# Loading two weight matrices in a permuted row order, in half-size transfers

## The chip, the cores and the metric

One core of one Trainium2 chip. The time is device time in microseconds of one execution. A run is called slow when it is over 1.5% above the fastest of the same kernel. Five runs here are slow (one of e3, one of e9, three of e10); every ratio and every profile of a whole kernel is of fast runs alone. The runs of one batch were made on one chip beside runs of the kernel before. A ratio compares the fast runs of two kernels in the same rounds and comes with a 95% interval; it is therefore not quite the ratio of the medians that stand beside it.

## The reference

Causal attention over 4 batches, 8 heads, 768 positions and head size 64 (three heads attend to everything, five to four sink positions and a window of 64), and then on x of 3072 x 512, the heads side by side:

```
h1 = x @ w1            # w1, w2: 512 x 1024
h2 = x @ w2
g = np.maximum(h1, h2)
out = g @ w_out        # w_out: 1024 x 512
```

## The kernel before

Since max(h1, h2) = h2 + relu(x (w1 - w2)), the kernel computes relu(x wd) w_out + x (w2 w_out) with wd = w1 - w2. A planner written in Python orders the instructions of all engines by estimated costs. The parts that matter here (cuts marked):

```python
def load_weight(name, c, queue=nc.sync):
    ...
    else:
        rows, cols = quarter(c)                # 256 rows, 512 columns
    queue.dma_start(out=dst[:, rows, cols],
                      in_=arr[rows.start * 128:rows.stop * 128, cols].rearrange("(c p) f -> p c f", p=128))
...
# wd = w1 - w2, a quarter at a time, on VectorE or GpSimd
    nc.vector / nc.gpsimd .tensor_sub(out=wd_bf[at], in0=w_raw[0][at], in1=w_raw[1][at])      # shortened
...
# w2 is cast to bf16, transposed on TensorE (8 groups) and multiplied by w_out
    nc.tensor.transpose(psb[:, c * 128:(c + 1) * 128], w2_bf[:, c, fch * 128:(fch + 1) * 128], ident)
...
# the attention result of a head, divided by its sum, goes into 64 columns of x
    V.tensor_tensor(out=xs[b].t[:, n0:n0 + nn, bass.ds(col(s0 + h), D)], in0=p4[:, i, :, 0:D],
                    in1=rz_[:, i].unsqueeze(2).to_broadcast([128, nn, D]), op=ALU.mult)
...
# x (w1 - w2): waits for the quarters of wd that hold its columns
    nc.tensor.matmul(bk.t[:, 0, 0:GT], lhsT=wd_bf[:, c, f * 128:(f + 1) * 128], rhs=xt[b].t[...], ...)
```

The softmax here doesn't subtract the row's maximum and nothing guards it: scores larger than these inputs give would overflow.

## Time and profile before

| | before |
|---|---|
| median of 4 runs, us | 187.32 (187.02 to 188.51) |
| TensorE busy in the profiled run | 170.2 of 186.1 us |
| DMA engines | full until about 125 us, then mostly free |
| w1 and w2 | 8 transfers of 512 KB, 7.5 us from issue to landing |

The views that bound the kernel stand in the prediction. One view is added: the chain that ended last, in order of time (start, length, what), here its longer pieces that carry the weights.

```profile
23.03 8.34 DMA raw<-in_moe_w_dram
31.39 7.52 DMA raw<-in_moe_w_dram
...
43.59 7.38 DMA raw<-in_moe_w_dram
51.05 2.45 POOL wd_bf L443 x2
```

The last quarter of w1 lands, and GpSimd at once subtracts w2 from it. In GpSimd's list (start, length, what, idle time before it and what ended it) its last two subtractions end at 55.7 us:

```profile
51.05 4.67 POOL L443 TENSOR_TENSOR wd_bf<-raw 128x1024 bf16<-128x1024 f32 x2 [0.61 <-DMA raw<-in_moe_w_dram]
```

In the list of TensorE's instructions the first product that needs this half of wd starts at 55.77 us.

### The profile page before, as it was taken

What the parts mean: (1) busy time and instruction counts of PE and PEld (TensorE: products, weight loads), DVE (VectorE), ACT (ScalarE), POOL (GpSimd) and SP (SyncE); (2) the same over time, 40 slices, a digit from 0 to 9 for tenths busy, and PEclk for the clock granted to TensorE, in tenths of its full rate; (3) what the DMA queues carried; (4) which work ended last, traced back from release to release, by engine and by line L of the source; (5) the groups of instructions that cost most, each with busy time, mean ns of one, the idle gap of its engine ahead of it and who ended that gap; (6) DMA issues with size and microseconds to landing.
All of it is one profiled execution on the core that took longest, in us unless ns stands there. A gap on an engine that the chain in (4) does not pass through costs nothing.

```text
span 186.1 us, 4594 instructions
## 1 busy us (share of the span) xinstructions
PE 170.2 (91%) x1643; PEld 100.6 (54%) x1663; DVE 88.0 (47%) x250; ACT 115.8 (62%) x195; POOL 50.7 (27%) x108
## 2 busy tenths in 40 slices
PE   1969988799999999999999999999999999999990
PEld 1845755556755655665565466446555545545460
DVE  5567775768778486544478165354743000000000
ACT  2546998878887678717894386368844624426330
POOL 2101331456796865623025234200000000000000
PEclk9985999999999999999999999999999999999999
DMA  6999999999999899999999999994016612022022
GB/s 142 303 272 356 288 335 354 248 289 311 324 255 249 187 223 221 239 239 176 262 227 240 237 207 202 331 175 174 5 58 188 96 60 113 0 80 89 4 113 70
DMA packets 79553, 36.96 MB, mean 199 GB/s; under 512 B 68642, under 2 KB 73506, under 8 KB 79522
## 3 DMA queue, kind: packets, MB, share of 16 engines
q1 hardware_dynamic: 76130, 35.27, 76.7%
q10 hardware_dynamic: 3392, 1.31, 2.7%
q8 instruction: 15, 0.25, 0.6%
q14 instruction: 16, 0.13, 0.2%
HBM read 25.17 MB, written 6.29 MB: 169 GB/s over the span
## 4 chain that ended last, share of the span: by engine, by line
PE 67%; DMA 15%; issue 4%; SPq 3%; POOL 2%; DVE 2%; DVEq 0%; ACT 0%; POOLq 0%
DMA raw<-in_moe_w_dram 12%; PE mm L786 12%; PE mm L762 10%; PE po L762 7%; PE po L623 7%; PE mm L793 6%; PE sc L578 6%; PE po L786 5%; PE sc L786 4%; DMA ld<-in_q_dram 3%; PE po L793 3%; PE sc L762 2%; PE sc L793 2%; SPq L671 2%; PE mm L695 1%
## 5 line engine op out<-in xcount | busy, mean ns | idle before, releaser
L599 ACT ACTIVATE at_all<-sc 128x1024 bf16<-128x1024 f32 (+2 forms) x72 | 59.8, 869 | 7.3 <-PE sc L578 3.6
L301 POOL CAST qb<-ld 128x384 bf16<-128x384 f32 x51 | 24.5, 508 | 25.1 <-DVE at_all L610 16.9
L762 PEld LDWEIGHTS <-wd_bf 128*128 128x128 bf16 x256 | 23.2, 98 | 14.4 <-POOL wd_bf L443 0.4
L762 PE MATMUL mm<-xt,wd_bf 128*128 128x384 bf16 x136 | 26.8, 326 | 0.2 <-POOL wd_bf L443 0.2
L623 PE MATMUL po<-vb,at_all 128*128 128x65 bf16 x472 | 26.6, 196 | 0.3 <-POOL vb L301 0.2
L623 PEld LDWEIGHTS <-at_all 128*128 128x128 bf16 x472 | 21.9, 99 | 9.0 <-issue 1.4
L578 PE MATMUL sc<-qk 64*128 64x128 bf16 (+2 forms) x364 | 23.1, 240 | 2.2 <-POOL qk L301 0.8
L642 DVE TENSOR_TENSOR xs<-po,rz 128x192 f32 x64 | 22.9, 357 | 2.9 <-DVE rz L639 0.6
L786 PEld LDWEIGHTS <-raw 128*128 128x128 bf16 x152 | 14.2, 98 | 13.8
L578 PEld LDWEIGHTS <-qk 64*128 64x128 bf16 x364 | 12.6, 95 | 14.7 <-issue 10.2
L786 PE MATMUL mm<-wo_bf,raw 128*128 128x512 bf16 (+1 forms) x75 | 18.9, 368 | 0.3
L301 POOL CAST vb<-ld 128x384 bf16<-128x384 f32 (+1 forms) x30 | 13.5, 475 | 20.8 <-DMA ld<-in_v_dram 8.8
L639 DVE RECIPROCAL rz<-po 128x6 f32<-128x6 f32 x32 | 6.2, 193 | 26.0 <-PE po L623 26.0
L762 PE MATMUL po<-xt,wd_bf 128*128 128x384 bf16 x92 | 18.1, 326 | 0.0
L299 ACT COPY ot<-mm 128x512 f32<-128x512 f32 (+1 forms) x12 | 6.8, 567 | 13.2 <-PE mm L793 11.6
L610 DVE TENSOR_TENSOR at_all<-at_all,smk 128x1024 bf16<-128x1024 bf16 (+3 forms) x27 | 14.9, 571 | 0.0
L793 PEld LDWEIGHTS <-xt 128*128 128x128 bf16 x100 | 9.3, 98 | 9.3
L793 PE MATMUL mm<-wm_bf,xt 128*128 128x512 bf16 (+1 forms) x55 | 13.9, 371 | 0.1
L610 DVE TENSOR_TENSOR at_all<-at_all,tri 128x256 bf16<-128x256 bf16 (+1 forms) x36 | 10.1, 313 | 6.6 <-ACT at_all L599 6.5
L695 PEld LDWEIGHTS <-qb 128*128 128x128 bf16 x108 | 7.2, 103 | 5.0 <-DVE qb L301 2.6
L299 ACT COPY vb<-vb 4x256 bf16<-4x256 bf16 (+1 forms) x16 | 6.1, 380 | 6.2 <-PE po L623 6.1
L770 ACT ACTIVATE raw<-mm 128x384 bf16<-128x384 f32 x17 | 8.3, 490 | 2.5 <-PE mm L762 2.2
(91 smaller groups left out, 188.5 us busy)
## 6 DMA issues: line engine op xcount, KB each, us to landing
ld<-in_q_dram SPq DMA_DIRECT2D x32, 192.0 KB, 4.9
ld<-in_k_dram SPq DMA_DIRECT2D x32, 192.0 KB, 4.6
out_dram<-ot SPq DMA_DIRECT2D x23, 256.0 KB, 2.5
ld<-in_v_dram SPq DMA_DIRECT2D x24, 192.0 KB, 4.0
raw<-in_moe_w_dram SPq DMA_DIRECT2D x8, 512.0 KB, 7.5
raw<-in_moe_w_out_dram SPq DMA_DIRECT2D x3, 512.0 KB, 5.8
xt<-in_v_dram ACTq DMA_DIRECT2D x3, 256.0 KB, 3.4
ld<-in_v_dram SPq DMA_DIRECT2D x8, 96.0 KB, 4.3
```

The costliest lines, as they stand in the source:

```text
L299: nc.scalar.copy(out=o, in_=i)
L301: issued[e].append((V if e == "DVE" else nc.gpsimd).tensor_copy(out=o, in_=i).ins)
L578: nc.tensor.matmul(sc.t[:, k, off:off + w], lhsT=qk.t[64 * h:64 * h + 64, 1, j * 128:(j + 1) * 128], rhs=qk.t[64 * h:64 * h + 64, 0, q0:q0 ...
L599: nc.scalar.activation(out=a.t[:, k:k + m, 0:n], in_=sc.t[:, k:k + m, 0:n], func=ACT.Exp, scale=scale, bias=0.0 if bias is None else bias[ ...
L610: issued["DVE"].append(V.tensor_mul(out=y, in0=y, in1=z).ins)
L623: nc.tensor.matmul(po[u].t[:, 0, o:o + D + 1], lhsT=a.t[:, k, off + t * 128:off + (t + 1) * 128], rhs=vb.t[:, h, j, :], **fresh(u))
L642: V.tensor_tensor(out=xs[b].t[:, n0:n0 + nn, bass.ds(col(s0 + h), D)], in0=p4[:, i, :, 0:D], in1=rz_[:, i].unsqueeze(2).to_broadcast([128, ...
L695: nc.tensor.transpose(psb[:, n * 128:(n + 1) * 128], qb.t[:, i, n].rearrange("p h d -> p (h d)"), ident)
L762: nc.tensor.matmul(bk.t[:, 0, 0:GT], lhsT=wd_bf[:, c, f * 128:(f + 1) * 128], rhs=xt[b].t[:, g * NB // NG:(g + 1) * NB // NG, c, :], start ...
L770: nc.scalar.activation(out=gt.t[:, f, :], in_=bk.t[:, 0, 0:GT], func=ACT.Relu)
L786: nc.tensor.matmul(bk.t[:, 0, 0:m1 - m0], lhsT=gt.t[:, f, t * 128:(t + 1) * 128], rhs=wo_bf[:, f, m0:m1], start=(f == 0), stop=False)
L793: nc.tensor.matmul(bk.t[:, 0, 0:m1 - m0], lhsT=xt[b].t[:, c0 // 128, c, :], rhs=wm_bf[:, c, m0:m1], start=False, stop=(c == KC - 1))
```

## The change

The intent, as I read it: let the DMA engines read neighbouring rows of w1 and w2 at the same time. The 128 rows of a chunk are taken in a two-level order, 16 groups of 8, row 16 b + a to partition 8 a + b. The rows are what x is multiplied along, so the columns of x must be permuted alike; pcol, the column of x at which a head's result starts, is computed by VectorE at run time and gets a new formula. Each quarter becomes two transfers of 256 KB.

```diff
+        rows, cols = quarter(c)
+        for r in range(rows.start, rows.stop):
+            queue.dma_start(out=dst[:, r, cols],
+                            in_=arr[r * 128:(r + 1) * 128, cols].rearrange("(b a) f -> a b f", a=16))
...
-        for o, width_ in ((perm, 1), (pcol, D)):
-            V.tensor_scalar_mul(out=o[0:1, 0:H], in0=key[0:1, 2, :], scalar1=-float(H * width_))
+        V.tensor_scalar_mul(out=perm[0:1, 0:H], in0=key[0:1, 2, :], scalar1=-float(H))
+        V.tensor_scalar(out=pcol[0:1], in0=perm[0:1, 0:H], scalar1=1, scalar2=None, op0=ALU.bitwise_and)
+        V.tensor_scalar_mul(out=key[0:1, 1, :], in0=perm[0:1, 0:H], scalar1=16.0)
+        V.scalar_tensor_tensor(out=pcol[0:1], in0=pcol[0:1], scalar=-15.0, in1=key[0:1, 1, :], op0=ALU.mult, op1=ALU.add)
...
-                        V.tensor_tensor(out=xs[b].t[:, n0:n0 + nn, bass.ds(col(s0 + h), D)], in0=p4[:, i, :, 0:D],
-                                        in1=rz_[:, i].unsqueeze(2).to_broadcast([128, nn, D]), op=ALU.mult)
+                        V.tensor_tensor(out=xs[b].t[:, n0:n0 + nn].rearrange("p n (y w) -> p n y w", w=4)[
+                        :, :, bass.ds(col(s0 + h), 16, 2)], in0=p4[:, i, :, 0:D].rearrange("p n (e a) -> p n a e", a=16),
+                                    in1=rz_[:, i].unsqueeze(2).unsqueeze(3).to_broadcast([128, nn, 16, 4]), op=ALU.mult)
```

(The planner's cost of a weight transfer goes from 0.5 to 1.0 us of SyncE; the bounds and the other branch follow the new column numbers.)

More of the change, by code (lines that the diff above doesn't have):

```diff
@@ L307, in load_weight @@
             rows, cols = slice(c * FC // 4, (c + 1) * FC // 4), slice(0, d_model)
-        else:
-            rows, cols = quarter(c)
-        queue.dma_start(out=dst[:, rows, cols],
-                          in_=arr[rows.start * 128:rows.stop * 128, cols].rearrange("(c p) f -> p c f", p=128))
+            queue.dma_start(out=dst[:, rows, cols],
+                            in_=arr[rows.start * 128:rows.stop * 128, cols].rearrange("(c p) f -> p c f", p=128))
+            return
+        rows, cols = quarter(c)
+        for r in range(rows.start, rows.stop):
+            queue.dma_start(out=dst[:, r, cols],
+                            in_=arr[r * 128:(r + 1) * 128, cols].rearrange("(b a) f -> a b f", a=16))
     def quarter(c):
@@ L425, in run @@
                 else:
-                    d_w[name, c] = P.op(lambda e, name=name, c=c: load_weight(name, c), {"SP": 0.5},
+                    d_w[name, c] = P.op(lambda e, name=name, c=c: load_weight(name, c), {"SP": 0.5 if name == "wo" else 1.0},
                                         prio=LATER[name, c], size=0.524, rate=0.35)
@@ L831 @@
     if not narrow:
-        run([True] * H, lambda s: s, lambda s: s * D, False)
+        run([True] * H, lambda s: s, lambda s: 32 * (s // 2) + s % 2, False)
         return
@@ L840 @@
         _, xcol = nc.values_load_multi_w_load_instructions(
-            pcol[0:1, 0:H], engines=(mybir.EngineType.DVE,), min_val=0, max_val=(H - 1) * D,
+            pcol[0:1, 0:H], engines=(mybir.EngineType.DVE,), min_val=0, max_val=32 * (H // 2 - 1) + 1,
             skip_runtime_bounds_check_because="a permutation of the heads")
@@ L844 @@
     with branch.Else():
-        run([True] * H, lambda s: s, lambda s: s * D, False)
+        run([True] * H, lambda s: s, lambda s: 32 * (s // 2) + s % 2, False)
         with tc.manual_schedule():
```

## The prediction

> **What bounds the kernel now.** I read four views, in this order: the busy times and the forty slices (what is full, and when), the stretches of time (how much TensorE idles in each part), the waits (what it idled for), and the DMA issues. First the page's busy line and slices (each digit is the busy share of 4.65 us in tenths):
>
> ```profile
> PE 170.2 (91%) x1643; PEld 100.6 (54%) x1663; DVE 88.0 (47%) x250; ACT 115.8 (62%) x195; POOL 50.7 (27%) x108
> ...
> PE   1969988799999999999999999999999999999990
> ...
> DMA  6999999999999899999999999994016612022022
> ```
>
> Two resources are full. TensorE is near nine tenths or above from the second slice to the end. The sixteen DMA engines are full from the second slice until about 125 us, then mostly free. The last third is dense matrix work with no loads to wait for. To put numbers on it I cut the span into stretches (length, then busy time and instructions of each engine, granted clock, DMA share, GB/s):
>
> ```profile
> 0.00:25.00 25.00, 17.86 (x203) 13.36 (x205) 15.93 (x57) 14.94 (x24) 5.44 (x23) 0.86 0.94 270
> 25.00:35.00 10.00, 7.58 (x117) 4.96 (x116) 7.13 (x17) 8.68 (x15) 1.23 (x4) 1.00 1.01 335
> 35.00:60.00 25.00, 24.41 (x299) 15.62 (x299) 18.91 (x48) 20.85 (x32) 18.30 (x29) 1.00 1.01 285
> 60.00:130.00 70.00, 69.36 (x708) 39.09 (x715) 38.16 (x109) 46.35 (x79) 25.68 (x56) 1.00 1.10 224
> 130.00:180.50 50.50, 50.23 (x324) 27.09 (x326) 7.86 (x21) 24.21 (x47) 0.00 (x0) 1.00 0.24 71
> ```
>
> TensorE idles 7.14 us before 25 us (4.19 of it before its first instruction), 2.42 us in 25 to 35, 0.59 in 35 to 60, 0.64 in 60 to 130 and 0.27 in 130 to 180.5. After 35 us a better transfer can return 1.5 us at most; the whole room in which weights can matter is 25 to 60 us, 3.0 us of idle time, 1.6% of the span. The waits of TensorE (total us, times, longest) say what these were:
>
> ```profile
> PE mm L401 <- DVE pcol L347: 4.2, 1, 4.2
> PE mm L695 <- DVE qb L301: 1.9, 3, 0.8
> PE mm L452 <- DVE w_bf L301: 0.9, 1, 0.9
> PE sc L578 <- POOL qk L301: 0.8, 1, 0.8
> ...
> PE mm L762 <- POOL wd_bf L443: 0.2, 1, 0.2
> ```
>
> Only the third and the last concern w1 and w2: 1.1 us. The first matters for another reason: nothing starts before VectorE has written pcol, and the diff makes pcol longer. The chain that ended last seems to contradict this small room:
>
> ```profile
> DMA raw<-in_moe_w_dram 12%; PE mm L786 12%; PE mm L762 10%; PE po L762 7%; PE po L623 7%; PE mm L793 6%; PE sc L578 6%; PE po L786 5%; PE sc L786 4%; DMA ld<-in_q_dram 3%; PE po L793 3%; PE sc L762 2%; PE sc L793 2%; SPq L671 2%; PE mm L695 1%
> ```
>
> 12% is 23 us of weight transfers on the chain. But they lie at 23.0 to 38.9 and 43.6 to 51.0 us, and in 35 to 60 TensorE was busy 24.41 of 25 us with other work. A chain names one sequence of releases; it does not say that TensorE stood still. I therefore do not take the 23 us as a gain to be had.
>
> [...] That is the motive I read into the diff: today neighbouring groups of partitions read w rows many 4 KiB pitches apart, and after it index a, the outermost, steps through adjacent rows. The trace of before does not show such a loss at this pitch. Its packet records give every 2,048-byte packet 84 ns in the median, for w1 and w2, for w_out (2 KiB rows, no gaps) and for the output alike. The means are 102.6 ns for the packets of 22.6 to 52 us (2,048 of w1 and w2, 256 of w_out) and 105 for the three w_out transfers before. [...] The new write of x puts runs of four bf16, 8 bytes,[...]; no row of before has this pattern. [...]
>
> **The change part by part.**
>
> ```profile
> L642 DVE TENSOR_TENSOR xs<-po,rz 128x192 f32 x64 | 22.9, 357 | 2.9 <-DVE rz L639 0.6
> ...
> L301 DVE COPY qk<-po 128x768 bf16<-128x768 bf16 x3 | 2.9, 954 | 1.7 <-PE po L623 0.9 <-POOL vb L301 0.8
> ...
> L301 DVE COPY xt<-po 128x768 bf16<-128x768 bf16 x1 | 0.6, 557 | 0.0
> ```
>
> *The multiply that writes x.* Same 64 instructions and 192 elements, but PSUM is read with steps of 16 floats in runs of four. The copy to qk reads PSUM with its innermost step over 256 bytes and takes 954 ns for 768 elements[...]; the copy to xt, which is contiguous, takes 557[...]. I expect 357 ns to stay, within 20 ns: 64 x 0.02 = 1.3 us at most, on an engine 47% busy. Nothing on the end.
>
> *The prologue.* Before, perm and pcol are two independent scalings starting 3.52 and 3.60 us into the trace and ending by 3.75. After, pcol is an AND of perm, a scaling of perm, and a combination: two instructions more, two dependent steps. Dependent small VectorE steps start 0.19 us apart here (2.88, 3.07, 3.26; 3.34 to 3.52), so AND at 3.71, scaling at 3.79, combination at 3.98, end at 4.13: 0.37 us later. The first load issues and TensorE's first instruction wait for it, so about +0.35 us on the path; a part may hide behind the w_out transfer already in the queue. I take +0.3.
>
> *The issues.* The page's issue rows (size, median time to landing):
>
> ```profile
> raw<-in_moe_w_dram SPq DMA_DIRECT2D x8, 512.0 KB, 7.5
> raw<-in_moe_w_out_dram SPq DMA_DIRECT2D x3, 512.0 KB, 5.8
> ```
>
> Eight issues become sixteen of 256 KB. One costs SyncE's queue about 0.47 us when it is not held, so 8 x 0.47 = 3.8 us more, spread over 21 to 47 us. In that stretch the queue was held by full DMA engines: issues of 2.71 us for two at 28.0, 2.88 for one at 31.4 and 2.68 for two at 43.6, against 0.47 each, which is 1.8 + 2.4 + 1.7 = 5.9 us of slack. The additional issues fit inside it. I take 0 for the end, with up to +0.5 if a q load falls behind.
>
> *The transfers.* Bytes, packet size and number of packets stay. The 7.5 us to landing is mostly backlog: 0.5 MB at about 300 GB/s is 1.7 us. The most that a better order can give is the mean falling to the median, (102.6 - 84) x 2,048 / 16 engines = 2.4 us of DMA time. As only 1.1 us of TensorE's idling was for these weights, and the excess looks the same for w_out, I take a tenth to a half of that: -0.3 us.
>
> *The schedule.* The kernel's own planner now reckons 1.0 us of SyncE for a weight transfer in place of 0.5. In its model the transfer itself takes 0.524/0.35 = 1.5 us, so the DMA stays the limit of its plan and the order should change little; a few swaps may shift the time by some tenths either way.
>
> Sum: 187.37 + 0.3 + 0 - 0.3 +- swaps = 187.4 us.
>
> **The rivals.** *Transfers were held by row conflicts, and the order frees them.* For it: the 23 us on the chain, 7.5 against 5.8 us to landing, packets of up to 1.08 us. Against it: the 84 ns median and the equal means. If the packets fell to 84 ns and all of the 1.1 us of weight waits and half of the other 25-to-35 us idle time went, the gain were about 1.8 us: 185.6. *The new grouping makes transfers slower.* [...] packets could near twice 84 ns, 2,048 x 84 / 16 = 10.8 us more DMA time before 52 us. TensorE would fill part of that with attention and lose perhaps 3 to 5 us: 190 to 192. Against it: nothing in before shows it, and how a 16 x 8 order is dealt to engines I cannot see. *VectorE becomes slower with the strided pattern*: at 200 ns more each, 12.8 us of VectorE work, of which perhaps 2 us in the first 60 us, where it is busy 17 of 25, delay TensorE: 189.
>
> **Range and chances.** The centre is 187.4. The first rival sets the low end, 185.6; half of the second's and all of the third's loss set the high end, 189.6. Faster by over 2% needs under 183.6, more than the 3.0 us of idle time before 60 us: 0.03. Slower by over 2% is above 191.1[...]: 0.08. Within 2%: 0.89.
>
> **What would show it.** Right: L642 stays at 357 ns; pcol ends about 0.37 us later and the first q load is issued that much later; sixteen weight issues with held issues shortened; 2,048-byte packets still 84 ns in the median; idle time of TensorE in 25 to 60 us between 2 and 3.5 us. Wrong: a packet median above 100 ns[...], a mean near 84 with weights landing earlier and the idle time under 1.5 us (conflicts), L642 above 400 ns, or an order of instructions that differs much on TensorE.

## The result

The changed kernel takes 193.97 us in the median of 4 runs (192.25 to 194.81) against 187.32 before: ratio 1.0341 (1.0264 to 1.0418). It is slower by 3.4%, outside the range on record. The result is correct.

The stretches of time of the kernel after (columns as in the prediction):

```profile
0.00:25.00 25.00, 17.99 (x204) 13.18 (x205) 16.47 (x59) 14.78 (x24) 5.75 (x22) 0.86 0.89 265
25.00:35.00 10.00, 7.68 (x114) 4.75 (x111) 5.17 (x12) 7.89 (x14) 0.75 (x3) 1.00 1.00 254
35.00:60.00 25.00, 21.59 (x247) 14.30 (x246) 17.10 (x38) 17.13 (x25) 13.38 (x22) 0.86 1.08 250
60.00:130.00 70.00, 68.33 (x702) 38.35 (x701) 41.53 (x114) 45.56 (x76) 30.32 (x60) 1.00 1.13 231
```

The last two columns tell the cause's place. In 25 to 35 us the DMA engines are as full as before (share 1.00 against 1.01), yet move 254 GB/s and not 335; in 35 to 60 us 250 and not 285. Full engines that move less are engines whose packets take longer: the weight packets took 122 ns in the median against 84, as counted below. TensorE idles 3.41 us in 35 to 60, where it had idled 0.59, and its granted clock there is 0.86: the record of the clock shows half of full speed for 6.8 us from 35.8 us on. Its waits:

```profile
PE mm L460 <- DVE w_bf L301: 2.7, 1, 2.7
...
PE mm L771 <- POOL wd_bf L451: 1.6, 1, 1.6
PE po L631 <- DVE xs L650: 1.2, 1, 1.2
```

The wait for the cast of w2 went from 0.9 to 2.7 us, that for wd from 0.2 to 1.6, and a new one stands on the multiply that writes x, which follows casts of late weights in VectorE's order. The multiply itself, and the page's row of weight transfers:

```profile
L650 DVE TENSOR_TENSOR xs<-po,rz 128x192 f32 x64 | 22.9, 357 | 2.8 <-DVE rz L647 0.6
...
raw<-in_moe_w_dram SPq DMA_DIRECT2D x16, 256.0 KB, 6.8
```

The multiply is as long as before. A transfer of half the size takes 6.8 us to land where the whole took 7.5; in e1 below, halves in plain order land in 4.9. The chain in order of time:

```profile
26.73 9.36 DMA raw<-in_moe_w_dram
36.11 6.94 DMA raw<-in_moe_w_dram
43.06 7.01 DMA raw<-in_moe_w_dram
...
53.70 6.62 DMA ld<-in_q_dram
...
60.51 2.35 POOL wd_bf L451
```

The chain names a q load before the last subtraction, but GpSimd's list shows that its two last subtractions run back to back and that w1 ended the wait before them:

```profile
58.20 4.65 POOL L451 TENSOR_TENSOR wd_bf<-raw 128x1024 bf16<-128x1024 f32 x2 [1.47 <-DMA raw<-in_moe_w_dram]
```

So it is the chain of before, later: GpSimd's last subtraction ends at 62.86 us, and the first product that needs it starts at 62.91, 7.14 us later than before. I then measured, in the profiled runs of the whole kernel, how long TensorE still works from this product to the start of its last instruction:

| run | transposes of w2, 5th group, us | that product of x wd, us | from there to TensorE's last start, us |
|---|---|---|---|
| before | 34.68 | 55.77 | 125.25 |
| after | 37.84 | 62.91 | 125.11 |
| e1_split | 34.29 | 55.11 | 124.88 |
| e3_form16far | 38.02 | 62.84 | 125.11 |
| e9_only_w2 | 37.77 | 59.61 | 124.88 |
| e11_only_w1 | 34.31 | 59.09 | 125.10 |
| e6_groups4 | 36.67 | 58.84 | 125.10 |
| e10_form4 | 35.00 | 56.57 | 125.24 |

The last column is constant within 0.4 us (in e2, e4 and e8, not in the table, it is 125.06, 124.88 and 125.24), so the column before it decides the time of the profiled run. The packet records of the two traces, counted over all weight packets of 2,048 bytes from 22.5 to 60 us (2,048 of w1 and w2, 256 of w_out), give the size: the median goes from 84 to 122 ns and the mean from 102 to 129. That is (129.0 - 102.3) x 2,304 / 16 engines = 3.8 us of DMA time. The packets of q and k (1,536 bytes), whose transfers the change does not touch, rise from 20.8 to 23.9 us of DMA time over the whole trace, 3.2 us more; of this 2.7 us (8.4 to 11.1) fall between the first and the last weight packet. Together 6.5 to 7.0 us, beside the 7.1 by which the product is late. This is an account of sizes and not a proof: the first weight packet also started 1.1 us later (22.65 and 23.72 us).

### The profile page after: what moved, and what is told of

It is laid out like the page before. It is cut to its first block, busy times and chain, and to the rows that moved or that the text cites.

```text
span 193.0 us, 4632 instructions
## 1 busy us (share of the span) xinstructions
PE 173.9 (90%) x1663; PEld 102.1 (53%) x1663; DVE 91.3 (47%) x252; ACT 116.1 (60%) x195; POOL 50.8 (26%) x108
## 4 chain that ended last, share of the span: by engine, by line
PE 65%; DMA 18%; SPq 5%; POOL 2%; issue 2%; DVE 1%; DVEq 0%; ACT 0%; POOLq 0%
PE mm L795 12%; DMA raw<-in_moe_w_dram 12%; PE mm L771 10%; PE po L771 7%; DMA ld<-in_q_dram 6%; PE po L631 6%; PE mm L802 6%; PE sc L586 6%; PE po L795 5%; PE sc L795 4%; SPq L315 4%; PE po L802 3%; PE sc L771 2%; PE sc L802 2%; PE mm L704 1%
## 5 line engine op out<-in xcount | busy, mean ns | idle before, releaser
L301 POOL CAST vb<-ld 128x384 bf16<-128x384 f32 (+1 forms) x30 | 13.7, 479 | 23.7 <-DMA ld<-in_v_dram 11.1
L795 PE MATMUL mm<-wo_bf,raw 128*128 128x512 bf16 (+1 forms) x80 | 19.4, 368 | 0.0
L647 DVE RECIPROCAL rz<-po 128x6 f32<-128x6 f32 x32 | 6.2, 193 | 24.1 <-PE po L631 23.9
L618 DVE TENSOR_TENSOR at_all<-at_all,tri 128x256 bf16<-128x256 bf16 (+1 forms) x36 | 12.5, 380 | 6.7 <-ACT at_all L607 6.6
L704 PEld LDWEIGHTS <-qb 128*128 128x128 bf16 x108 | 7.7, 106 | 6.0 <-DVE qb L301 2.5
```

Source lines behind the costliest of these rows:

```text
L301: issued[e].append((V if e == "DVE" else nc.gpsimd).tensor_copy(out=o, in_=i).ins)
L618: issued["DVE"].append(V.tensor_mul(out=y, in0=y, in1=z).ins)
L704: nc.tensor.transpose(psb[:, n * 128:(n + 1) * 128], qb.t[:, i, n].rearrange("p h d -> p (h d)"), ident)
L795: nc.tensor.matmul(bk.t[:, 0, 0:m1 - m0], lhsT=gt.t[:, f, t * 128:(t + 1) * 128], rhs=wo_bf[:, f, m0:m1], start=(f == 0), stop=False)
```

## The experiments

Three things changed in the transfers at once: their number, which rows are read together, and the form of the source order. Theory P supposes that the form, 16 groups of 8 partitions, makes the packets slow, because DMA engines then hinder each other at the partitions they write; e7 calls it the port theory. Theory H supposes that neighbouring rows, read at once, collide in HBM, the memory that the inputs lie in. S says that the number of transfers costs it, X that the writing of x does. For every kernel of the whole-kernel experiments the order of TensorE's instructions was compared with that of before and is the same (e8 has its added products besides). Before itself took 186.57 us in the median in the batch of e1 to e4, 187.20 in that of e6 to e9, and 186.99 in that of e10 and e11.

### e1_split: the number of transfers alone

```diff
+        for r in range(rows.start, rows.stop):
+            queue.dma_start(out=dst[:, r, cols], in_=arr[r * 128:(r + 1) * 128, cols])
```

> The kernel before with nothing but each weight transfer cut in two (256 KB each, rows in their natural order, sixteen issues as in the changed kernel); right results. Theory P[...] and theory H (neighbouring rows are read at once and collide in HBM) both expect about 187.5 us, 2,048-byte packets of the weights near 84 ns in the median and 24 us idle of nothing new. Theory S (sixteen transfers of half the size cost it: more issues[...]) expects 193 to 195 us with packets still at 84 ns.

Measured: correct, 186.61 us (186.14 to 187.68), ratio 0.999 (0.9921 to 1.0059). Packets 84 ns in the median, mean 99, and a transfer lands in 4.9 us. Eight more issues cost nothing that can be seen: all sixteen take SyncE 9.2 us, the eight of before 9.4. S falls.

### e2_xonly: the columns of x and the prologue alone

```diff
 # the changed kernel with the load of before
+        queue.dma_start(out=dst[:, rows, cols],
+                        in_=arr[rows.start * 128:rows.stop * 128, cols].rearrange("(c p) f -> p c f", p=128))
```

> The changed kernel with the weights loaded as before (eight transfers, natural row order); the columns of x stay permuted, so the result is wrong on purpose. P, H and S expect 187.0 to 188.0 us, the multiply that writes x at 357 ns. Theory X (the strided write of x and the longer pcol cost it) expects 193 to 195 us.

Measured: wrong, 187.33 us (187.11 to 188.05), ratio 1.0035 (0.9975 to 1.0096). The multiply takes 357 ns here too. X falls as the cause; a cost of some tenths of a per cent is neither shown nor excluded.

### e3_form16far: the two-level order, rows far apart

```diff
 # e1 with another source: group a starts 7 rows after group a-1
+  bass.AP(tensor=arr.tensor, offset=r * 128 * d_ff + cols.start, ap=[[7 * d_ff, 16], [d_ff, 8], [1, d_ff // 2]])
```

> Sixteen transfers as in e1, but each source is a two-level order of 16 groups of 8 rows, group a starting 7 rows after group a-1 and its 8 rows following one another, so that groups lie 28 KiB apart and not 4 KiB as in the changed kernel; wrong result on purpose (rows 7 a + b). P expects the loss of the changed kernel, 193 to 195 us, with weight packets of 105 to 140 ns in the median. H expects about 187.5 us and 84 ns.

Measured: wrong, 193.9 us in the median of 6 (192.68 to 195.67, one of them slow; 193.03 without it), ratio 1.0314 (1.0238 to 1.039). Packets 118 ns in the median. This is the whole loss, with the groups 28 KiB apart and not 4. TensorE's waits are those of after:

```profile
PE mm L455 <- DVE w_bf L301: 3.0, 1, 3.0
PE mm L765 <- POOL wd_bf L446: 1.8, 1, 1.8
```

### e4_near128: neighbouring rows, plain order

```diff
 # e1 with another source: one level, 1 KiB from partition to partition
+  bass.AP(tensor=arr.tensor, offset=r * 128 * d_ff + cols.start, ap=[[d_ff // 4, 128], [1, d_ff // 2]])
```

> Sixteen transfers as in e1 in the plain one-level order over 128 partitions, but with a step of 1 KiB and not 4 KiB from partition to partition[...]; wrong result on purpose. P expects about 187.5 us and packets of 84 ns. H expects 193 to 195 us and packets of 105 to 140 ns.

Measured: wrong, 187.04 us (186.27 to 187.6), ratio 0.9993 (0.9932 to 1.0055), packets 84 ns, mean 98.5. Together e3 and e4 decide between P and H: the form (16 groups of 8) costs the time, and the distance of the rows does not. H falls as the cause of this loss for the distances tried: 4 and 28 KiB from group to group (122 and 118 ns a packet), 4 and 1 KiB from partition to partition (84 ns both). How the form does it is not shown by them.

### e5_alone: transfers with nothing beside them

Eight loads of one form at a time, each batch waiting for the last. This is one execution, its state unknown.

> No attention and no products: eight loads of 256 KB (128 KB for low) of w1 at a time, with nothing beside them, in nine forms one after another; wrong result on purpose. nat and tail are the plain order; adjs is that of the changed kernel (16 groups of 8, groups 4 KiB apart); fars has groups 28 KiB apart; near is the plain order with a 1 KiB step; low fills partitions 0 to 63 alone; gfour is 32 groups of 4, gtwo 64 groups of 2; same has all 16 groups read the same 8 rows. P expects nat, near and tail at 84 ns a packet, some 360 GB/s; adjs, fars, gfour and same slow alike, 105 to 150 ns; low[...] slow too[...]; gtwo between. H expects adjs and near slow, same the slowest, fars at 84 ns.

Measured: packet medians of 84 ns for nat, near and tail, 119 for adjs and 118 for same, as P expected. In the steady middle of a batch adjs starts about 65 packets per half microsecond, near about 89. Three expectations were missed. The median of fars is 84 ns (above 100 in parts of its batch, mean 110, against 118 for adjs). That is what H expected and not P; near at 84 ns speaks against H all the same. In the whole kernel the two distances hardly differ (e3 118 ns, after 122), so a small effect of the distance beside that of the form stays open. gfour and gtwo have a median of 84 ns and a 90th percentile of 84 and 85: a two-level order is not slow as such, groups of eight are (adjs and same here, e3 in the kernel). And low has 84 ns, but its issues limited it: 128 KB per issue, and an issue took 0.62 us. A by-product is the cost of an issue, from SyncE's list (start, length of all eight, what):

```profile
9.68 3.65 SPq L36 DMA_DIRECT2D nat<-in_moe_w_dram  x8
19.79 5.14 SPq L40 DMA_DIRECT2D adjs<-in_moe_w_dram  x8
...
49.76 4.99 SPq L52 DMA_DIRECT2D low<-in_moe_w_dram  x8
57.23 5.10 SPq L56 DMA_DIRECT2D gfour<-in_moe_w_dram  x8
```

Over all 128 partitions a two-level source takes 5.14/8 = 0.64 us to issue, a plain one 0.46. The two levels are not all that counts: low has a plain source too, to 64 partitions, and takes 0.62.

### e6_groups4: the same idea with groups of four rows

```diff
-  arr[r * 128:(r + 1) * 128, cols].rearrange("(b a) f -> a b f", a=16)
+  arr[r * 128:(r + 1) * 128, cols].rearrange("(b a) f -> a b f", a=32)     # x in runs of 2, pcol = 32 perm - 31 (perm & 1)
```

> The changed kernel with 32 groups of 4 rows in place of 16 groups of 8: row 32 b + a goes to partition 4 a + b, and the columns of x follow; sixteen transfers in two-level order as in the changed kernel, right result. If groups of eight partitions[...] (theory P, narrowed after e5, where groups of 4 and 2 kept 84 ns), this takes 186.5 to 188 us with packets at 84 ns. If any two-level order, or its dearer issue (0.63 us against 0.46 in e5), costs the time, it takes 192 to 195 us.

Measured: correct, 189.39 us in the median of 6 (188.54 to 190.84), ratio 1.0107 (1.0077 to 1.0137). Packets are back at 84 ns, mean 105 (102 before). Both expectations missed: two thirds of the loss are gone, and 1.1% stays.

### e7_ports: the partitions

The transfers alone again, of whole 4 KiB rows, to chosen partitions; one execution, its state unknown.

```diff
+    batch("mids", 32, 64, [[3 * W, 16], [W, 4]], 64)     # 16 groups of 4, to partitions 32 to 95
+    batch("lows", 0, 64, [[3 * W, 16], [W, 4]], 64)      # the same to partitions 0 to 63
```

> Transfers alone again, now of whole 4 KiB rows so that issues do not limit them; wrong result on purpose. mids and lows are the same 16 groups of 4 rows, to partitions 32 to 95 and 0 to 63; midp and lowp the same in plain order; eight is 16 groups of 8 on 128 partitions, four 32 groups of 4, plain the plain order. The port theory expects[...] mids near 165 ns a packet of 4 KiB and 390 GB/s while it runs steadily[...], lows[...], lowp like lows, midp like mids, eight between (200 to 280 ns), four and plain near 165. If it is the slowest dimension of 16 that is slow, mids, lows and eight are slow alike and lowp is not.

Measured, 4,096-byte packets:

| batch | order, partitions | median ns | mean ns |
|---|---|---|---|
| mids | 16 groups of 4, 32 to 95 | 159 | 192 |
| lows | 16 groups of 4, 0 to 63 | 324 | 302 |
| midp | plain, 32 to 95 | 159 | 187 |
| lowp | plain, 0 to 63 | 318 | 296 |
| eight | 16 groups of 8, all 128 | 272 | 260 |
| four | 32 groups of 4, all 128 | 159 | 180 |
| plain | plain, all 128 | 159 | 194 |

The page's rows of transfers say the same in us to landing:

```profile
eight<-in_moe_w_dram SPq DMA_DIRECT2D x6, 512.0 KB, 8.5
four<-in_moe_w_dram SPq DMA_DIRECT2D x6, 512.0 KB, 6.9
plain<-in_moe_w_dram SPq DMA_DIRECT2D x6, 512.0 KB, 6.1
...
mids<-in_moe_w_dram SPq DMA_DIRECT2D x6, 256.0 KB, 4.1
lows<-in_moe_w_dram SPq DMA_DIRECT2D x6, 256.0 KB, 5.2
midp<-in_moe_w_dram SPq DMA_DIRECT2D x6, 256.0 KB, 4.0
lowp<-in_moe_w_dram SPq DMA_DIRECT2D x6, 256.0 KB, 4.9
```

mids and lows differ in nothing but the partitions, and the packets of lows take twice as long: 324/159 = 2.04. The plain orders lowp and midp show the same, 318 and 159 ns. P expected lows and lowp to be the slow ones. So in this run it was the 64 partitions written that decided what a packet cost, in either order. The rival, that a slowest dimension of 16 is slow as such, falls: mids has it and keeps 159 ns. Sixteen groups of eight show 1.71 times the time of the plain order on the same 128 partitions (272 against 159 ns), within what P expected, and groups of four show no such rise (159 ns). All of this fits DMA engines that hinder each other where they write. That remains the author's reading: no record names the engine of a packet, and how a source order is dealt to the engines was not shown.

### e8_filler: work for TensorE in its longest gap

```diff
+                for _ in range(FILL if fch == FC // 2 else 0):        # FILL = 24
+                    nc.tensor.matmul(bk.t[:, 0, 0:128], lhsT=ident, rhs=ident, start=True, stop=True)
```

> The changed kernel with 24 matrix products of the identity put before the fifth group of transposes of w2, where TensorE idles 2.7 us; right result. If the half clock that follows this idle time (6.8 us of it) is a separate part of the loss, the clock stays at full and the time falls by 1.5 to 2.5 us, to 191.5 to 192.5. If the half clock costs nothing, or is not caused by the idle time, 193.5 to 194.5.

Measured: correct, 193.57 us (192.32 to 194.17), ratio 1.033 (1.0287 to 1.0372) to before, against 1.0341 for the kernel after. In the profiled runs the stretch of half clock shrank from 6.8 to 3.4 us, but it did not vanish, and the time is that of after. So the half clock is not shown to be a separate part of the loss where both matrices are slow. e11 explains why that is plausible: with w1 alone slow, the product of x wd is late by 3.3 us without any half clock, because wd is late; time won on TensorE before it is then waited away.

### e9_only_w2 and e11_only_w1: the order of groups of eight on one matrix

```diff
 # e3, with the source chosen by name
+  <two-level order of e3> if name == "w2" else arr[r * 128:(r + 1) * 128, cols]      # e11: "w1"
```

> e3 with the two-level order for w2 alone, w1 in the plain order; wrong result on purpose. In the trace of the changed kernel the transposes of w2 start 3.2 us later than before, the half clock adds about 2, and the waits for w1's part come to 1.6 us. If these three add up, this run takes 190.5 to 192.5 us; if only the total of slow transfers counts, half of the loss, about 190.

> The other half of e9: the groups of 8 for w1 alone; wrong result on purpose. e9 (w2 alone) lost 2.3% of the 3.3%. If the two losses add, this loses 0.8 to 1.3%, 188.7 to 189.7 us, with TensorE waiting for the difference of weights and not for w2. If either alone costs most of it, 2% or more.

Measured, both wrong: w2 alone 191.95 us (190.48 to 194.17, one of four slow; 191.46 without it), ratio 1.023 (1.0175 to 1.0284), within what was expected if the parts add. w1 alone 190.81 us (189.49 to 191.23), ratio 1.0164 (1.011 to 1.0218), more than expected. The two losses sum to 3.9% where both together cost 3.1% (e3); the intervals are too wide to tell whether they overlap. In the profiled runs the delays of the product of x wd add up: 3.8 us (e9) and 3.3 (e11), against 7.1 in e3. w2 delays the transposes by 3.1 us and w1 leaves them alone, as the table above shows; both end in the same product of x wd, by different ways. In e11 this product waits 1.3 us for wd. In e9 it waits for nothing: TensorE itself comes late, being busy 29.9 us from 25 us to this product against 27.9 before, with 3.4 us at half clock among them, and idle 4.7 against 2.8. With w2 alone the half clock thus probably costs time, at most 1.7 us (half of 3.4, an estimate).

### e10_form4: the two-level order with groups of four, x untouched

```diff
 # e1 with another source
+  bass.AP(tensor=arr.tensor, offset=r * 128 * d_ff + cols.start, ap=[[3 * d_ff, 32], [d_ff, 4], [1, d_ff // 2]])
```

> e1 (natural x, sixteen transfers) with a two-level source of 32 groups of 4 rows; wrong result on purpose. It separates what is left of e6: e6 was 1.1% slower with packets at 84 ns. If the dearer issue of the two-level order (about 0.63 us against 0.48, sixteen times, 2.4 us of SyncE's queue) is what is left, this is 0.7 to 1.1% slower than before, 188.5 to 189.3 us. If it is the permuted x and the longer pcol, this equals e1, within 0.3% of before.

Measured: wrong, 189.1 us in the median of 18 (187.48 to 191.62, three of them slow; 188.7 without them), ratio 1.0089 (1.0064 to 1.0114), with packets at 84 ns in the median and 103 in the mean (102 before). What stays in e6 thus comes, for the most part, with the two-level order and not with x. SyncE's list of weight issues, first e1, then e10:

```profile
21.54 1.91 SPq L313 DMA_DIRECT2D raw<-in_moe_w_dram  x4
...
23.97 2.18 SPq L313 DMA_DIRECT2D raw<-in_moe_w_dram  x4
```

```profile
21.43 2.60 SPq L313 DMA_DIRECT2D raw<-in_moe_w_dram  x4
...
24.72 2.59 SPq L313 DMA_DIRECT2D raw<-in_moe_w_dram  x4
```

The sixteen issues take 12.1 us in e10 and 9.2 in e1, and the product of x wd starts 1.5 us later than in e1. That fits a dearer issue, as expected; no run kept the two-level order and made its issue cheap, so this part rests on the fit.

## Why the prediction was wrong

- **The step that failed is the transfers: "I take a tenth to a half of that: -0.3 us."** In its place stands a loss: weight packets at 122 ns in the median, against 84 before, cost 3.8 us of DMA time and the q and k packets beside them 2.7 to 3.2. The prediction named slower transfers in the new grouping as its second rival and gave a loss of over 2% a chance of 0.08, because "nothing in before shows it". That was no evidence: before loads no weights in such an order, so it could not have shown it. e3 and e4 show that the order is the cause; e7 shows that packets to partitions 0 to 63 take 2.04 times as long as those to 32 to 95, and that on all 128 partitions groups of eight take 1.71 times as long as the plain order. That DMA engines hinder each other in the changed order is the reading that fits, inferred and not recorded. The rival's sizes were off as well: packets rose by 45% in the median and not twofold, the untouched q and k transfers also paid, and the time came to 194 and not 190 to 192.
- **The reading of the bound was half right.** Idle time of 3.0 us in 25 to 60 us does limit what faster weights can give. It says nothing about what slower weights cost. The chain said so: it ran through w1, GpSimd's subtraction and the product of x wd, and TensorE waited 0.2 us for wd, which means no slack at all. I dismissed the chain because TensorE was busy beside it; from that product on TensorE has 125 us of work that cannot start earlier.
- **The issues: "I take 0 for the end".** True for the number of transfers (e1, ratio 0.999). Their form is another matter: a two-level source takes 0.64 us to issue and not 0.47, and e10 lost 0.9%, which this fits. The prediction had no term for it.
- **The prologue: +0.3 us was wrong, the traces show 0.** pcol came 0.39 us later, as worked out, but the first q load was issued at 4.85 us in both traces and TensorE started at 4.19 and 4.20. Something else held these by then; which, I did not trace.
- **The multiply that writes x, at 357 ns, and the schedule were right.** That it would keep the 357 ns of before was the estimate; the trace of after shows it, 357 ns in the mean of 64. No instruction of TensorE, ScalarE or GpSimd changed its place.
- **The first rival (row conflicts in HBM, which the change would free) did not come true**: e1 and e4 leave packets at 84 ns and the time as it was, whether the rows step by 4 KiB from partition to partition or by 1. So the motive of the change found no support.
- **A small slip of a number:** the mean of the weight packets of before is 102.3 ns and not 102.6; the most that a better order could give stays at 2.3 to 2.4 us.

What stays open: the engine that a packet ran on, and with it how groups of eight come to cost more; the exact part of the issue in the last 0.9%; the share of TensorE's half clock; and why fars alone (e5) was faster than adjs.

## What to carry to other kernels

The order in which a source is written does not only say which bytes go where; here it also decided what a packet costs (84 ns or 122), and in e7 the partitions that it goes to did so too (159 ns or 324). So time such an order alone, with nothing beside it, before building on it. A wait of 0.2 us on the chain that ended last is not small change but zero slack: ask what every instruction behind it would do if it came later. And where a rival concerns something that the kernel before does not contain, its absence from the trace is no argument against it.
